# Second products of the late expert units in two blocks instead of four

## Chip, cores and metric

The kernel runs on one core of a Trainium2 chip. The metric is the device time of one execution in microseconds (us), as the median of repeated runs. Matrix products run on TensorE (PE in the profile, its weight loads PEld), elementwise work on VectorE (DVE), ScalarE (ACT) and GpSimd (POOL); SyncE (SP) issues the DMAs.

## The reference, cut to what matters

A sparse attention (4 x 8 heads, 576 tokens, 64 wide) gives `x` with 2304 tokens of 512. Two mixture stages follow; the change lies in the last one:

```python
def _moe2_ref(x, w_gate, w1, w2):
    ...
    for e in range(E):                    # E = 8 experts
        h = np.maximum(x @ w1[e], 0.0)    # 512 -> 1024, the "first products"
        ye = h @ w2[e]                    # 1024 -> 512, the "second products"
        out += P[:, e:e + 1] * ye
    return out
```

## The kernel before, in words

Attention comes first, then the first mixture (24 units "a" and "b"), then 96 expert units. A unit is (e, s, j): expert e of 8, block s of three blocks of 768 tokens, quarter j of the 1024 hidden columns. They are numbered after the 24 units: unit 24 + 32 s + 4 e + j, with s outermost. `Moe.run` (L886) writes out the order of all engines by hand: each engine executes its instructions in the order in which they are issued there.

A unit has seven **slots**. In each slot `mm1` (L684) issues six matmuls of 384 columns into one of two PSUM banks: slots 0, 2 and 4 write `px`, slots 1, 3, 5 and 6 write `py` (`SLOTS`, L521). Slot 2 adds onto what slot 0 left in `px`, and slot 6 onto what slot 5 left in `py`; slots 1, 3, 4, 5 and slot 0 start their bank anew. `combine` (L710) reads the bank after each slot:

- slot 0: ACT copies `px` to `p1` (L716; `p` in the profile).
- slot 1: DVE adds `py` and `p1` into `u2` (L719; `u`).
- slot 2: ACT makes `hh` of `px` (L757), and in slot 3 DVE makes `hl` of `px` (L758).
- slot 3: DVE adds `py` and `u2` into `v` (L722).
- slots 4, 5 and 6: DVE adds the bank and `v` or `u2` into `c` (L736), ACT makes `hh` of `c`, and DVE later makes `hl` of `c` and `hh`, two operands that both lie in SBUF.

So `py` can be started anew in slot 3 only when DVE has read it for `u2`, and `px` can be added to in slot 2 only when ACT has read it for `p1`.

The **second products** of a unit are a queue of 36 matmuls of 512 columns (`queue_d`, L791), which are issued in the next unit, behind the first products of some slots. `pop` (L820) takes a share of the columns left, by the row of `POPS` (L41) that holds for the unit:

```python
POPS = ((1, 1, 1, 1, 1, 2, 1), (0, 2, 0, 2, 0, 3, 1))
...
        n = sum(q[0] for q in self.queue) * share / max(share, self.left)
        self.left -= share
        while self.queue and (n > 0 or not self.queue[0][0]):
...
            self.pops = POPS[u >= 8 * NSB + 16]
```

The second row holds from unit 40 on, which is expert 4 of the first block (the fifth one), to unit 119: 80 units. Its shares 2, 2, 3 and 1 of 8 give blocks of 9, 9, 14 and 4 matmuls behind slots 1, 3, 5 and 6.

When the queue belongs to j = 3, each of the six token tiles ends with `accumulate` (L805), 128x512 on DVE (L816), for expert 0 on ACT instead (L812). `pop` puts these aside in `late`, and at the start of each slot at most two are taken, to be issued at the end of that slot:

```python
                late, self.late = self.late[:2], self.late[2:]
                self.mm1(u, slot)
                ...
                self.pop(slot)
                self.evac(u, slot)
                ...
                for f in late:
                    f()
```

They run in the units with j = 0 and at the start of those with j = 1. Beside all this the weights of the next unit are prepared: `prep1` (L592) on ACT and POOL (L607 to L619), one step in each of slots 0 to 4, and `prep2` (L632), a `w2h` on ACT in slot 3 and a `w2l` on DVE (L642) in slot 5. In the last unit of a block and the first of the next, `xsplit` (L676) adds an `xh` on ACT (L680) and an `xl` on DVE (L681) to slots 0 to 3, and 1 to 3.

Of the kernel before, what the change touches and what calls it, by code (L numbers as in the profile page):

```python
# [37 lines left out]
ORDER = ('wsmTqSfVIviocylrezgxtX', 'msiTSzyVfcqgxwretIXvol', 'imsTSvofwcgIezxltrqyVX', 'TmszVreSviyocxIgfqtlXw', 'mTIVqySvorzseliwcfgxtX', 'msTwVfiSeocyIvgzxlqrtX', 'omTreVfzSqgxwvltXyIcis', 'wmTsSfxvryeiqlVzoIXctg', 'gmTSiVzreIvcofxqlwtsXy', 'miVogTqSvsIcwzyexfrtXl', 'gTmysiSrewfoVcqzxIXtvl', 'VolTsqymiSwcgzfxIvretX', 'mTfoSvcireyszVgxqwtIXl', 'lmszycVTIeoiwfvSgxrtqX', 'ymlTsqwcreVoSfvIzgxtXi', 'moTeSscqzgxyfwVlIvrtXi', 'ymzwoTigSvqxfcreIlsVXt', 'TmSrleIvVzosfcwgxitXqy')  # L38
LOAD_AT, KEYS_AT = 1, 5
PD = 2  # L40
POPS = ((1, 1, 1, 1, 1, 2, 1), (0, 2, 0, 2, 0, 3, 1))  # L41
AHEAD = {-16: 1, -15: 1, -14: 1, -13: 1, -12: 3, -11: 0, -10: 0, -9: 0, -8: 0, -7: 0, -6: 3, -5: 0, -4: 0, -3: 0, -2: 2, -1: 0, 0: 1, 1: 3, 2: 3, 3: 1, 4: 1, 5: 0, 6: 1, 7: 2}
RAMP = 4
CHUNKS = "owooooo3o3o333w3ww3w3w3w3w33ww33ww3ww3ww"
# [471 lines left out]
class Moe:  # L516
# [319 lines left out]
    def gate(self, s, slot):  # L836

        ps = self.xy[0 if slot == 6 else 1]
        t0 = slot - 2
        for tc in (t0, t0 + 1):  # L840
            t = SB * s + 128 * tc
            for d in range(4):
                self.nc.tensor.matmul(ps[:, E * tc:E * tc + E], lhsT=self.x[:, d, t:t + 128], rhs=self.wg[:, d],  # L843
                                      start=d == 0, stop=d == 3, skip_group_check=True)

        def out():
            self.nc.scalar.activation(self.p[:, 6 * s + t0:6 * s + t0 + 2],
                                      ps[:, E * t0:E * t0 + 2 * E].rearrange("p (a b) -> p a b", a=2), AF.Copy)
        return out
# [36 lines left out]
    def run(self):  # L886
        units = self.units
        prep = self.prep1(0)
        for i in range(4):
            self.xsum(0, i, self.nc.vector)  # L890
            next(prep, None)
            yield
        for _ in prep:
            yield
        for slot in range(4):
            while not self.rooms:
                yield
            self.xsplit(0, slot)
            yield
        while self.xy is None or self.pool is None:  # L900
            yield
        sink = None
        gates = {8 * s + (12 if s + 1 < NSB else 9): s for s in range(NSB)}
        for u, (kind, s, j) in enumerate(units):
            nxt = units[u + 1] if u + 1 < len(units) else None
            while u == 1 and self.pool2 is None:
                yield
            if kind != "a":
                self.hs[u] = tuple(self.pool2.tile([128, 2, SB], F32R, tag=t, name=f"{t}{u}", bufs=2)
                                   for t in ("hh", "hl"))  # L910
            ahead = [units[min(u + i, len(units) - 1)][1] for i in range(5)]
            splits, turns = {0: 4, 1: 5, 2: 6} if u == 0 else {}, {}
            if kind == "b" and ahead[1] != s:
                turns = {i + 1: i for i in range(4)}
            elif u and units[u - 1][0] == "b" and units[u - 1][1] != s:
                splits = {i - 3: i for i in range(4, 7)}
            elif ahead[1] != s:
                splits = dict(SPLITS_AT)
            elif u and units[u - 1][1] != s:
                splits = {at - 7: slot for at, slot in SPLITS_AT}  # L920
            prep = self.prep1(u + 1)
            self.load1(u + 2)
            self.pops = POPS[u >= 8 * NSB + 16]
            for slot in range(7):
                yield
                late, self.late = self.late[:2], self.late[2:]
                self.mm1(u, slot)
                gate = self.gate(gates[u], slot) if u in gates and slot in (2, 4, 6) else None
                if sink:
                    try:  # L930
                        sink.send(self.xy[0 if slot in (2, 4, 5) else 1])
                    except StopIteration:
                        sink = None
                self.pop(slot)
                self.evac(u, slot)
                if gate:
                    gate()
                    if u == 8 * NSB + 1 and slot == 6:
                        sink = self.sinkhorn()
                        next(sink)  # L940
                for f in late:
                    f()
                if slot in splits:
                    self.xsplit(ahead[1], splits[slot])
                next(prep, None)
                at = 4 if u == 7 else 1
                if u < 8 and slot in (at, at + 1):
                    self.keep(u, slot - at)
                if slot in turns:
                    self.xturn(u // 8 if kind == "b" else u // 8 - 1, turns[slot])  # L950
                if kind in ("a", "b"):
                    if slot in XSUMS.get(u % 8, ()):
                        self.xsum(NEXT_SB[u // 8], u % 8 - 2 + XSUMS[u % 8].index(slot), self.nc.vector)
                    for at, x in STAGED.get(u % 8, ()):
                        if slot == at:
                            self.xstage(u // 8, x, at // 3 % 2)
                elif slot == 5 and ahead[4] != s:
                    self.xsum(ahead[4], next(i for i in range(4) if ahead[3 - i] == s), self.nc.gpsimd)
                if slot in (3, 5):
                    self.prep2(u + 1 if kind == "a" else u, (slot - 3) // 2)  # L960
            while self.later:
                self.later.pop(0)()
            if kind == "b":
                self.queue_b(u)
                self.left = (2 if nxt[0] == "a" else 1) * sum(self.pops)
            elif kind != "a":
                self.queue_d(u)
                self.left = sum(self.pops)
        self.left = 0
        self.pop(6)  # L970
        for f in self.late:
            f()
# [64 lines left out]
```

## Time and profile before

| | |
|---|---|
| Median of 3 runs | 2189.16 us (2189.15 to 2190.59) |
| The profiled execution | 2189.07 us, span 2187.3 us |
| TensorE | 2150.1 us busy, 98% of the span |
| DVE, ACT, POOL | 58%, 43%, 48% |
| Granted TensorE clock | 1.00 |
| Expert units, first matmul of unit 24 to the end | from 676.4 us on |

The span runs from the first to the last instruction; the time of the execution is 1.8 us longer. Rows of the timeline give start, duration, engine, line, and out<-in of an instruction, all in us from the start of the span. The duration of a matmul holds its way through the array, which overlaps with the next one, so the pace of TensorE is read from the distance between starts.

### The profile page before, as it was taken

What the parts mean: (1) busy time and instruction counts of PE and PEld (TensorE: products, weight loads), DVE (VectorE), ACT (ScalarE), POOL (GpSimd) and SP (SyncE); (2) the same over time, 40 slices, a digit from 0 to 9 for tenths busy, and PEclk for the clock granted to TensorE, in tenths of its full rate; (3) what the DMA queues carried; (4) which work ended last, traced back from release to release, by engine and by line L of the source; (5) the groups of instructions that cost most, each with busy time, mean ns of one, the idle gap of its engine ahead of it and who ended that gap; (6) DMA issues with size and microseconds to landing.
All of it is one profiled execution on the core that took longest, in us unless ns stands there. A gap on an engine that the chain in (4) does not pass through costs nothing.

```text
span 2187.3 us, 31994 instructions
## 1 busy us (share of the span) xinstructions
PE 2150.1 (98%) x12496; PEld 1872.5 (86%) x12496; DVE 1274.8 (58%) x2122; ACT 948.0 (43%) x1770; POOL 1042.4 (48%) x1018
## 2 busy tenths in 40 slices
PE   7999999999999999999999999999999999999999
PEld 4666666899999899999998999999998999999998
DVE  7888888765555654454556445454546444545454
ACT  7888887442324333333334333333334333333332
POOL 6665657740003444444456545454456444444441
PEclk9999999999999999999999999999999999999999
DMA  4333442775552212121212121212112221212121
GB/s 154 105 128 123 133 139 86 260 264 188 222 199 105 78 58 77 59 77 59 77 58 93 72 77 58 77 59 77 64 72 73 92 72 63 77 59 78 58 77 39
DMA packets 64183, 218.09 MB, mean 100 GB/s; under 512 B 6944, under 2 KB 11040, under 8 KB 64032
## 3 DMA queue, kind: packets, MB, share of 16 engines
q1 hardware_dynamic: 64032, 216.05, 28.0%
q8 instruction: 98, 1.61, 0.3%
q14 instruction: 53, 0.43, 0.1%
HBM read 185.61 MB, written 30.41 MB: 99 GB/s over the span
## 4 chain that ended last, share of the span: by engine, by line
PE 90%; DVE 7%; ACT 2%; issue 1%; POOL 0%; DMA 0%; SPq 0%; ACTq 0%; DVEq 0%; POOLq 0%
PE ye L762 40%; PE py L692 22%; PE px L692 17%; PE s L143 4%; PE pv L241 2%; PE t L187 2%; DVE p L162 2%; DVE nmx L147 2%; PE w L474 1%; DVE cva L506 1%; PE py L843 0%; PE tt L198 0%; ACT e L155 0%; DVE cva L503 0%; PE rb L271 0%
## 5 line engine op out<-in xcount | busy, mean ns | idle before, releaser
L762 PE MATMUL ye<-w2l,hh 128*128 128x512 f32 x1152 | 450.6, 391 | 0.0
L762 PE MATMUL ye<-w2h,hl 128*128 128x512 f32 x1152 | 450.5, 391 | 0.0
L762 PE MATMUL ye<-w2h,hh 128*128 128x512 f32 x1152 | 449.6, 390 | 0.0
L757 ACT ACTIVATE hh<-c 128x384 fp32r<-128x384 f32 x288 | 151.2, 526 | 621.4 <-DVE c L736 621.4
L619 POOL TENSOR_TENSOR w1l<-wt,w1h 128x1024 fp32r<-128x1024 f32 x104 | 253.2, 2434 | 267.2 <-ACT w1h L616 267.1
L692 PE MATMUL py<-xh,w1h 128*128 128x384 f32 x960 | 322.6, 336 | 2.4 <-DVE c L736 1.2
L692 PE MATMUL py<-xh,w1l 128*128 128x384 f32 x960 | 322.1, 336 | 0.0
L692 PE MATMUL py<-xl,w1h 128*128 128x384 f32 x960 | 321.9, 335 | 0.0
L614 POOL TENSOR_TENSOR w1l<-raw,w1h 128x256 fp32r<-128x256 f32 x104 | 80.4, 773 | 471.2 <-ACT w1h L608 457.8
L762 PEld LDWEIGHTS ye<-w2h,hl 128*128 128x128 f32 x1152 | 216.2, 188 | 40.5
L762 PEld LDWEIGHTS ye<-w2l,hh 128*128 128x128 f32 x1152 | 216.3, 188 | 35.3 <-DVE w2l L642 0.3
L692 PE MATMUL px<-xh,w1h 128*128 128x384 f32 x720 | 242.0, 336 | 1.5 <-ACT p L716 1.5
L762 PEld LDWEIGHTS ye<-w2h,hh 128*128 128x128 f32 x1152 | 216.3, 188 | 30.7
L692 PE MATMUL px<-xl,w1h 128*128 128x384 f32 x720 | 241.6, 336 | 0.0
L692 PE MATMUL px<-xh,w1l 128*128 128x384 f32 x720 | 241.5, 335 | 0.0
L607 POOL TENSOR_TENSOR wt<-raw 128x512 f32<-128x512 f32 x104 | 140.8, 1354 | 198.0 <-DMA raw<-in_e 183.0
L758 DVE SCALAR_TENSOR_TENSOR hl<-c,hh 128x384 fp32r<-128x384 f32 x288 | 189.3, 657 | 9.5
L692 PEld LDWEIGHTS py<-xh,w1h 128*128 128x128 f32 x960 | 180.3, 188 | 14.8 <-DVE c L736 3.5
L692 PEld LDWEIGHTS py<-xl,w1h 128*128 128x128 f32 x960 | 180.3, 188 | 7.7
L736 DVE TENSOR_TENSOR c<-px,v 128x384 f32<-128x384 f32 x108 | 60.0, 556 | 212.8 <-PE px L692 212.7
L692 PEld LDWEIGHTS py<-xh,w1l 128*128 128x128 f32 x960 | 180.3, 188 | 0.0
L758 DVE SCALAR_TENSOR_TENSOR hl<-px,hh 128x384 fp32r<-128x384 f32 x96 | 53.4, 556 | 215.5 <-ACT hh L757 215.4
(144 smaller groups left out, 3941.0 us busy)
## 6 DMA issues: line engine op xcount, KB each, us to landing
raw<-in_e SPq DMA_DIRECT2D x192, 512.0 KB, 4.0
wraw<-in_w SPq DMA_DIRECT2D x32, 512.0 KB, 4.0
w1h<-w_kept SPq DMA_DIRECT2D x16, 896.0 KB, 5.2
w1l<-w_kept SPq DMA_DIRECT2D x16, 896.0 KB, 7.0
rq<-in_qk SPq DMA_DIRECT2D x15, 576.0 KB, 5.7
w_kept<-w1h SPq DMA_DIRECT2D x8, 896.0 KB, 8.2
w_kept<-w1l SPq DMA_DIRECT2D x8, 896.0 KB, 9.3
raw<-w SPq DMA_DIRECT2D x12, 512.0 KB, 3.6
```

The source lines that it names most:

```text
L143: nc.tensor.matmul(out[:, c, 0:KH], lhsT=q[rows, g, cols], rhs=kk[rows, g], start=True, stop=True)
L147: nc.vector.tensor_reduce(out=nmx[:, s % 18:s % 18 + 1], in_=ps[:, :, 0:288], axis=AX.XY, op=ALU.max, negate=True)
L162: nc.vector.scalar_tensor_tensor(out=ppool[g][:, i, 0:S].rearrange("p (a b) -> p a b", a=2), in0=ps[:, :, 0:288], scalar=thr[:, s % 18:s % ...
L187: nc.tensor.transpose(ps[:, c], p[:, 128 * c:128 * c + 128], k.ident)
L607: nc.gpsimd.tensor_tensor(out=t[:, 0:2], in0=raw[:, 1:3], in1=raw[:, 0:2], op=ALU.subtract)
L614: nc.gpsimd.tensor_tensor(out=wl[:, 0], in0=raw[:, 0], in1=f32(wh[:, 0]), op=ALU.subtract)
L619: nc.gpsimd.tensor_tensor(out=wl[:, 3:7], in0=t, in1=f32(wh[:, 3:7]), op=ALU.subtract)
L692: self.nc.tensor.matmul(out, lhsT=w[:, wi, o], rhs=x[xi][:, d], start=n == 0 and not adds, stop=n == 5, skip_group_check=True)
L736: tt(out=c, in0=src, in1=add, op=ALU.add)
L757: nc.scalar.activation(hi, src, AF.Relu)
L758: self.later.append(lambda: nc.vector.scalar_tensor_tensor(out=lo, in0=src, scalar=0.0, in1=f32(hi), op0=ALU.max, op1=ALU.subtract))
L762: self.queue.append((out.shape[-1], lambda: self.nc.tensor.matmul(out, lhsT=l, rhs=r, start=start, stop=stop, skip_group_check=True)))
```

## The change

The second row of `POPS` gets shares 4.5 and 3.5 behind slots 3 and 5 (the fourth and sixth slot) and none elsewhere. 18432 columns x 4.5 / 8 are 10368, so the first block takes 21 matmuls of 512 columns, the second the other 15. As this row has no share in slot 6 any more, the flush behind the last unit takes the first row.

```diff
-POPS = ((1, 1, 1, 1, 1, 2, 1), (0, 2, 0, 2, 0, 3, 1))
+POPS = ((1, 1, 1, 1, 1, 2, 1), (0, 0, 0, 4.5, 0, 3.5, 0))
...
-        self.left = 0
+        self.left, self.pops = 0, POPS[0]
         self.pop(6)
```

## Rows read from the trace of the kernel before

**Rows 1.** The page: 40 slices of the span (busy tenths, clock), the chain by engine.
```profile
PE   7999999999999999999999999999999999999999
...
PEclk9999999999999999999999999999999999999999
...
PE 90%; DVE 7%; ACT 2%; issue 1%; POOL 0%; DMA 0%; SPq 0%; ACTq 0%; DVEq 0%; POOLq 0%
```

**Rows 2.** Windows: length, busy time (instructions) of PE, PEld, DVE, ACT, POOL; clock; DMA.
```profile
809.39:933.76 124.37, 124.37 (x625) 112.39 (x624) 60.29 (x99) 42.24 (x73) 57.91 (x48) 1.00 0.20 68
933.76:1181.76 248.00, 248.00 (x1249) 224.73 (x1248) 128.62 (x187) 87.29 (x148) 128.66 (x99) 1.00 0.19 68
...
1181.76:1197.95 16.19, 15.93 (x79) 13.90 (x78) 14.03 (x18) 7.37 (x12) 10.26 (x8) 1.00 0.32 114
```

**Rows 3.** Timeline of PE, units 64 and 65: last matmuls of slot 6 and slot 0.
```profile
1320.86 0.34 PE L692 MATMUL py<-xh,w1l 128*128 128x384 f32 x1
...
1322.81 0.34 PE L692 MATMUL px<-xh,w1l 128*128 128x384 f32 x1
```

**Rows 4.** Timeline of DVE from the end of unit 64 into unit 65.
```profile
1321.23 0.56 DVE L736 TENSOR_TENSOR c<-py,u 128x384 f32<-128x384 f32 x1 [0.88 <-PE py L692]
1321.70 0.55 DVE L758 SCALAR_TENSOR_TENSOR hl<-c,hh 128x384 fp32r<-128x384 f32 x1
1322.17 0.74 DVE L816 SCALAR_TENSOR_TENSOR acc<-ye,prob,acc 128x512 f32<-128x512 f32 x1
1322.83 0.55 DVE L758 SCALAR_TENSOR_TENSOR hl<-c,hh 128x384 fp32r<-128x384 f32 x1
1323.30 1.40 DVE L816 SCALAR_TENSOR_TENSOR acc<-ye,prob,acc 128x512 f32<-128x512 f32 x2
1324.62 0.55 DVE L719 TENSOR_TENSOR u<-py,p 128x384 f32<-128x384 f32 x1
```

**Rows 5.** Timeline of PE, unit 1, which has no second products between its slots.
```profile
400.23 0.34 PE L692 MATMUL py<-xh,w1l 128*128 128x384 f32 x1
...
401.27 0.34 PE L692 MATMUL px<-xh,w1l 128*128 128x384 f32 x1
...
402.48 0.34 PE L692 MATMUL px<-xh,w1h 128*128 128x384 f32 x1
...
403.52 0.34 PE L692 MATMUL py<-xh,w1h 128*128 128x384 f32 x1
...
407.46 0.44 PE L692 MATMUL py<-xh,w1h 128*128 128x384 f32 x1 [0.65 <-DVE c L736]
```

**Rows 6.** Timeline of DVE: unit 1, unit 55, and the end of unit 63.
```profile
402.74 0.56 DVE L719 TENSOR_TENSOR u<-py,p 128x384 f32<-128x384 f32 x1 [1.57 <-PE py L692]
...
406.85 0.56 DVE L736 TENSOR_TENSOR c<-py,v 128x384 f32<-128x384 f32 x1
...
1169.70 0.55 DVE L719 TENSOR_TENSOR u<-py,p 128x384 f32<-128x384 f32 x1
...
1301.97 0.90 DVE L758 SCALAR_TENSOR_TENSOR hl<-c,hh 128x384 fp32r<-128x384 f32 x1
```

**Rows 7.** Timeline of POOL: the end of unit 63, the start of unit 65.
```profile
1301.71 0.74 POOL L610 TENSOR_TENSOR wt<-raw,wt 128x256 f32<-128x256 f32 x1
1302.53 0.93 POOL L613 TENSOR_TENSOR wt<-raw,wt 128x256 f32<-128x256 f32 x1
...
1324.12 0.75 POOL L614 TENSOR_TENSOR w1l<-raw,w1h 128x256 fp32r<-128x256 f32 x1 [5.33 <-ACT w1h L608]
```

**Rows 8.** Timeline of ACT: units 55, 60 to 61, and 65.
```profile
1167.57 0.49 ACT L716 ACTIVATE p<-px 128x384 f32<-128x384 f32 x1 [0.90 <-PE px L692]
...
1259.82 0.53 ACT L757 ACTIVATE hh<-c 128x384 fp32r<-128x384 f32 x1 [3.17 <-DVE c L736]
1260.25 0.67 ACT L812 ACTIVATE acc<-ye,prob 128x512 f32<-128x512 f32 x1
...
1323.25 0.49 ACT L716 ACTIVATE p<-px 128x384 f32<-128x384 f32 x1 [0.90 <-PE px L692]
```

## The prediction

> **What bounds the kernel now.** I read the page first. The chain that ended last is TensorE's for 90% [rows 1], so only what changes TensorE's pace, or makes it wait, moves the time. Then the windows of the stretch that the change touches: sixteen units from 933.76 to 1181.76 us take 248.00 us, 15.50 each, and TensorE is busy in all 248.00 [rows 2]. There is no wait to remove. The eight units before them, which run on the other row of `POPS` with seven blocks a unit, take 124.37 us, 15.55 each, also without a gap [rows 2]. The same 78 matmuls thus cost 0.047 us more with seven blocks than with four: 0.0155 us for each block. That is all that blocks cost by themselves.
>
> Last I read the timelines around the start of a unit, since the change takes the cover away there. In the kernel before, 4 second products lie between slot 6 and slot 0, and 9 between slot 1 and slot 2. In the kernel after, slots 6, 0, 1, 2 and 3 stand back to back: 4 x 6 matmuls after slot 6 and slot 3 begins.
>
> **The change, part by part.** All offsets count from T, the start of the last matmul of slot 6.
>
> *Fewer blocks.* Two of four go in each of 80 units: 80 x 2 x 0.0155 = 2.5 us saved. Each matmul, weight load, elementwise instruction and DMA is still issued, the same number of times. SP's loads keep their place in the unit; the output DMAs move with their accumulations by a slot or so, and the loads behind them are needed a unit later, so that costs nothing while that unit of 15.5 us lasts. POOL's queue is not reordered; its steps only start with ACT's copies, and what they make is needed a unit later.
>
> *Where slots 0 to 3 would start.* Unit 1 is a unit without second products, so its slots already stand as the change puts them: from T = 400.23 the last matmul of slot 0 starts at 401.27, slot 2 at 402.48 and slot 3 at 403.52 [rows 5]. That is T + 1.04, T + 2.25 and T + 3.29, with no wait.
>
> *Units that follow no accumulation (58 of 80, the two at the edges set aside).* `u2` must be ready before slot 3. In unit 1 it ran from T + 2.51 to T + 3.07 [rows 6], 0.22 us before slot 3. In the late units the DVE queue ahead of it is `c`, `hl`, `hl`, which are done by about T + 2.1 (`c` starts at T + 0.37, the two `hl` follow, 0.55 each, the last held until `hh` is made) [rows 3, 4, 8]. I cost these at nothing; the cover is those 0.2 us.
>
> *Units that follow an accumulation (j = 1).* Here lies the cost. Behind slot 6 the DVE of the kernel before issues `c`, `hl`, one accumulation, `hl`, two accumulations, and only then `u2`, which starts at 1324.62, T + 3.76 with T = 1320.86, and ends at T + 4.31 [rows 3, 4]. Nobody notices, since nine second products stand between slot 1 and slot 2. The change keeps three accumulations there: the last three tiles end in the block of 15 behind slot 5, slot 6 takes two of them and the next unit's slot 0 the third. The order becomes `c`, `hl`, `acc`, `acc`, `hl`, `acc`, `u2`; the sum of the intervals is the same 3.39 us from `c` to `u2`, and DVE has no gap in it. So `u2` ends at T + 4.31 or later, while slot 3 would start at T + 3.29. TensorE waits there with everything behind it: slot 3, then the block of 21.
>
> *One more delay in that chain.* With slot 0 right behind slot 6, ACT's `p1` starts 0.44 after slot 0's last matmul [rows 3, 8], at T + 1.48, and POOL's L614 starts 0.87 after `p1` [rows 7, 8], at T + 2.35, until T + 3.10. In the kernel before it came at T + 3.26, behind the second `hl`. Now this `hl` starts at T + 2.63 (0.37 + 0.47 + 0.47 + 0.66 + 0.66 from the starts in [rows 4]), inside L614. A pair of the kind is in the trace: an `hl` that started 0.26 into POOL's L610 took 0.90 and ended 0.42 after it, in place of 0.55, and POOL's next, L613, took 0.93 meanwhile [rows 6, 7]; so DVE gets its turn before the POOL instruction behind. Hence `hl` ends at T + 3.52 and not at T + 3.18, `u2` at T + 4.65. The Trainium skill's page "SBUF — State Buffer", section "Who interferes with whom", says that a VectorE instruction with two SBUF operands and a GpSimd one that reads SBUF exclude each other, and that the second blocks until the first is through. By that rule the whole 0.55 would follow L614, for an `hl` until T + 3.65, 18 x 0.13 = 2.3 us more in the sum; the row shows 0.42, and I take the row.
>
> *The wait itself.* The one like it in unit 1: `c` ended at 407.41 and the matmul that waited started at 407.46, and shows 0.44 where its neighbours show 0.34 [rows 5, 6]. I take 0.05 for the release and 0.10 for the restart. A stall is 4.65 + 0.05 + 0.10 - 3.29 = 1.51 us. Bounds: without the POOL delay and the restart 4.31 + 0.05 - 3.29 = 1.07; with twice the release and restart 1.66. I take 1.51, as each of its parts has a row.
>
> *How many.* Accumulations fall into units 40, 44, ..., 116, so 20 units follow one. For 18 of them it is DVE's: 18 x 1.51 = 27.2 us. Units 61 and 93 follow expert 0, whose accumulations run on ACT, 0.67 each behind an `hh`, the first 0.43 after it [rows 8]. Two of them now precede `p1`: `hh` at T + 0.96 (its `c` ends at T + 0.93), `acc` at 1.39 and 2.06, `p1` at 2.73 to 3.22, and slot 2 needs it at 2.25: 0.97 + 0.15 = 1.1 us each, 2.2 in all (0 if ACT's order hid it).
>
> *Edges.* In units 55 and 87 an `xl` stands ahead of `u2`, which started 2.13 after `p1` [rows 6, 8]: T + 3.61, ending at 4.16, a stall of 4.16 + 0.15 - 3.29 = 1.0 each, 2.0 us. Unit 56 takes 16.19 us, 0.69 above the rest [rows 2], and unit 88 is its twin. One accumulation of the block behind slot 1 leaves the DVE queue before slot 5, so I give back 0.5 of each: -1.0 (between 0 and -1.4).
>
> **Sum:** 27.2 + 2.2 + 2.0 - 2.5 - 1.0 = +27.9 us on the profiled execution's 2189.07, which is 0.09 below the median of the runs shown: **2217 us**, 1.3% slower. With the low stall the sum is 18 x 1.07 + 2.2 + 2.0 - 2.5 - 1.4 = +19.6, 2208.7; with the high one and no return at the edges +31.6, 2220.7.
>
> **Rivals.**
> *The stall does not come, and only the blocks count.* This ends on the other side. The place is the DVE queue between slot 6 and `u2`; it decides at T + 3.24, the latest end of `u2` that slot 3 doesn't feel. If accumulations were through before `c`, the queue would be that of the other units, and the time 2189.07 - 2.5 - 1.0 = 2185.6 if the edges don't stall either. For it: before, this very queue harmed nobody. Against it: the block of 15 ends only one slot before, at most two accumulations are taken in a slot, and the 3.39 us are back to back in the trace. Chance 0.07.
>
> *Every unit stalls a little.* The 58 others have 0.2 us to spare in slot 3, and less than that in slot 1, whose `py` waits for the `c` of slot 6 (T + 0.93, slot 1 at T + 1.21). If `hl` or `hh` came later by 0.4, each would lose some 0.2 us: 58 x 0.2 = 12 us more, 2229. Against it is unit 1, whose slots had just such cover and did not wait [rows 5]. The Trainium skill's page "Perfetto Trace Analysis", section "Matmuls", speaks for it: groups of matmuls should rotate through PSUM banks so that the evacuation of one overlaps the next, and the change stacks five slots on two banks. Chance 0.10.
>
> *The clock falls after the stalls.* TensorE's clock was granted in full in each slice, the first included, in which it was busy for seven tenths only [rows 1]. Stalls of 1.5 us in 62 are less idle time than that; chance 0.02, and no row prices it.
>
> *The change reaches other units than I say.* The words speak of the third expert; the code's unit 40 is the fifth. From the third, two more stalls would come: 2220, inside the range.
>
> **How the numbers follow.** The forecast has 0.81, the rivals 0.07, 0.10 and 0.02. The range reaches from 2206, somewhat below the low stall, to 2224, above the high one and half way into the second rival; it leaves out the first rival and the rest of the second. A measurement of this kernel can tell some 0.2%, 4.4 us, from no change. The first rival at 2185.6 is 0.16% faster, so within it, save for a small chance that more is gained: same 0.06, faster 0.02, slower 0.92.
>
> **What would show it.** The list of waits should have a new row, `py` L692 waiting for DVE's `u` L719, some 20 times, about 1.3 us of idle time each, in the units with j = 1 only, and one of `px` waiting for ACT's `p` in units 61 and 93. Units with j = 0, 2 and 3 should take 15.47 us, those with j = 1 about 17.0. In units with j = 1 the `hl` behind two accumulations should last about 0.9 us, with L614 beside it. The forecast is wrong if that row is missing, if the waits stand in all units, or if the other units do not come down to 15.47.

## The result, and the profile after

The changed kernel takes 2219.19 us (median of 4 runs, 2218.57 to 2219.66) against 2189.66 us of the kernel before beside it: 1.013 times as long, with a 95% interval of 1.0118 to 1.0142. The profiled execution took 2218.57 us, its span is 2216.8 us. The predicted 2217 us stand 2.2 us below the median.

The page of the kernel after, TensorE's row of busy time and the chain (before: [rows 1]):

```profile
PE 2154.1 (97%) x12496; PEld 1872.3 (84%) x12496; DVE 1217.0 (55%) x2122; ACT 946.5 (43%) x1770; POOL 1024.5 (46%) x1018
...
PE 86%; DVE 10%; ACT 2%; issue 1%; DMA 0%; POOL 0%; SPq 0%; ACTq 0%; DVEq 0%; POOLq 0%
```

The number of instructions is the same; TensorE's share of the chain fell from 90% to 86%, and DVE's rose from 7% to 10%. What took TensorE's place is in the list of waits of TensorE from 930 us on (waiting for whom: us in total, times, longest):

```profile
PE py L692 <- DVE u L719: 23.6, 20, 1.2
PE px L692 <- ACT p L716: 1.3, 2, 0.7
```

Both rows are new in this stretch, and there are no others: 20 waits of `py` for `u2`, two of `px` for `p1`. The kernel before has one row there, which is gone, for slot 6 of units 56 and 88:

```profile
PE py L692 <- DVE c L736: 0.5, 2, 0.3
```

The windows put them into units. The first four are units 64 to 67 (j = 0 to 3), then units 55, 56 and 61; the columns are those of [rows 2]:

```profile
1315.68:1331.18 15.50, 15.50 (x79) 14.07 (x79) 7.82 (x13) 5.26 (x9) 7.17 (x6) 1.00 0.13 51
1331.18:1348.16 16.98, 15.75 (x79) 13.99 (x79) 8.00 (x13) 5.26 (x9) 7.46 (x6) 1.00 0.23 80
1348.16:1363.67 15.51, 15.51 (x79) 14.08 (x79) 5.94 (x10) 5.26 (x9) 7.17 (x6) 1.00 0.19 69
1363.67:1379.14 15.47, 15.47 (x79) 14.04 (x79) 5.93 (x10) 5.27 (x9) 7.16 (x6) 1.00 0.20 65
...
1172.70:1189.20 16.50, 15.75 (x80) 14.00 (x79) 13.05 (x14) 8.21 (x13) 11.84 (x7) 1.00 0.12 46
1189.20:1204.71 15.51, 15.51 (x80) 14.08 (x80) 12.67 (x16) 7.46 (x12) 8.15 (x6) 1.00 0.32 119
1268.17:1284.56 16.39, 15.74 (x79) 13.99 (x79) 5.93 (x10) 6.90 (x12) 7.13 (x6) 1.00 0.18 61
```

Of the first four only the unit with j = 1 has a gap: 16.98 us, of which TensorE is busy 15.75. The same window shows the full clock. The cause stands in the timelines of unit 65. DVE of the kernel after, where [rows 4] showed the kernel before:

```profile
1331.39 0.56 DVE L736 TENSOR_TENSOR c<-py,u 128x384 f32<-128x384 f32 x1 [0.90 <-PE py L692]
1331.86 0.55 DVE L758 SCALAR_TENSOR_TENSOR hl<-c,hh 128x384 fp32r<-128x384 f32 x1
1332.33 1.40 DVE L816 SCALAR_TENSOR_TENSOR acc<-ye,prob,acc 128x512 f32<-128x512 f32 x2
1333.64 0.87 DVE L758 SCALAR_TENSOR_TENSOR hl<-c,hh 128x384 fp32r<-128x384 f32 x1
1334.44 0.74 DVE L816 SCALAR_TENSOR_TENSOR acc<-ye,prob,acc 128x512 f32<-128x512 f32 x1
1335.10 0.54 DVE L719 TENSOR_TENSOR u<-py,p 128x384 f32<-128x384 f32 x1
```

POOL in the same stretch:

```profile
1333.36 0.74 POOL L614 TENSOR_TENSOR w1l<-raw,w1h 128x256 fp32r<-128x256 f32 x1 [7.40 <-ACT w1h L608]
1334.05 1.60 POOL L617 TENSOR_TENSOR w1l<-raw,w1h 128x512 fp32r<-128x512 f32 x1
```

And TensorE, the last matmuls of slots 6 and 2, the first two of slot 3:

```profile
1331.01 0.34 PE L692 MATMUL py<-xh,w1l 128*128 128x384 f32 x1
...
1334.13 0.34 PE L692 MATMUL px<-xh,w1l 128*128 128x384 f32 x1
1335.70 0.45 PE L692 MATMUL py<-xh,w1h 128*128 128x384 f32 x1 [1.23 <-DVE u L719]
1335.98 0.34 PE L692 MATMUL py<-xl,w1h 128*128 128x384 f32 x1
```

T is 1331.01. `u2` ends at 1335.64, T + 4.63, and slot 3 starts 0.06 later, where it would have started at T + 3.29. Read the second `hl`: it starts 0.28 into L614, takes 0.87 in place of 0.55 and ends 0.41 after L614 does. Read the restart: the second matmul comes 0.28 after the first, where 0.17 is the pace.

From unit 40 to the end the change adds 28.9 us (1282.5 against 1253.5). By units: 18 x (16.98 - 15.50) = 26.6, units 61 and 93 2 x 0.89 = 1.8, units 55 and 87 2 x 1.00 = 2.0, units 56 and 88 -1.3, all others together -0.2. The 0.6 us that the two executions differ by ahead of unit 40 lie in unit 5, which the change does not touch.

### The profile page after: what moved, and what is told of

It reads as the page before. It is cut to its first block, busy times and chain, and to the rows that moved or that the text cites. A ratio compares the mean times of both kernels' runs of the same rounds, so it can differ in the third digit from the quotient of the medians.

```text
span 2216.8 us, 31994 instructions
## 1 busy us (share of the span) xinstructions
PE 2154.1 (97%) x12496; PEld 1872.3 (84%) x12496; DVE 1217.0 (55%) x2122; ACT 946.5 (43%) x1770; POOL 1024.5 (46%) x1018
## 4 chain that ended last, share of the span: by engine, by line
PE 86%; DVE 10%; ACT 2%; issue 1%; DMA 0%; POOL 0%; SPq 0%; ACTq 0%; DVEq 0%; POOLq 0%
PE ye L762 39%; PE py L692 21%; PE px L692 15%; PE s L143 4%; PE pv L241 2%; PE t L187 2%; DVE p L162 2%; DVE acc L816 2%; DVE nmx L147 1%; PE w L474 1%; DVE hl L758 1%; DVE cva L506 1%; DVE c L736 1%; PE py L843 0%; PE tt L198 0%
## 5 line engine op out<-in xcount | busy, mean ns | idle before, releaser
L614 POOL TENSOR_TENSOR w1l<-raw,w1h 128x256 fp32r<-128x256 f32 x104 | 79.8, 768 | 680.5 <-ACT w1h L608 666.6
L758 DVE SCALAR_TENSOR_TENSOR hl<-c,hh 128x384 fp32r<-128x384 f32 x288 | 168.1, 584 | 9.5
L736 DVE TENSOR_TENSOR c<-py,u 128x384 f32<-128x384 f32 x108 | 60.1, 557 | 171.3 <-PE py L692 171.1
```

The source lines that it names most:

```text
L614: nc.gpsimd.tensor_tensor(out=wl[:, 0], in0=raw[:, 0], in1=f32(wh[:, 0]), op=ALU.subtract)
L736: tt(out=c, in0=src, in1=add, op=ALU.add)
L758: self.later.append(lambda: nc.vector.scalar_tensor_tensor(out=lo, in0=src, scalar=0.0, in1=f32(hi), op0=ALU.max, op1=ALU.subtract))
```

## The experiments

The theory: DVE's three accumulations ahead of `u2` make slot 3 wait, where no second products stand between slots 1 and 3. The first rival: the stacked slots make TensorE wait by themselves. The second, on one term of the sum: no instruction of POOL holds `hl`, and the chain is the sum of its intervals. The ratios are to the kernel before.

**The accumulations behind `u2`.** The blocks stay as the change has them.

```diff
-                late, self.late = self.late[:2], self.late[2:]
+                n = 0 if slot in (6, 0) and self.pops is POPS[1] else 2
+                late, self.late = self.late[:n], self.late[n:]
```

> The change's two blocks stay, but no accumulation is issued in slot 6 or slot 0 of the late units, so the last three of a tile group stand behind u2 on DVE (and behind p1 on ACT). Theory (three accumulations ahead of u2 make slot 3 wait): the 18 stalls of 1.5 us and the 2 of 0.9 go, units with j = 1 take 15.5 us in place of 16.98, 2219.2 - 28.7 = 2190.5 us; the stalls of 1.0 us in units 55 and 87 stay. Rival (five stacked slots on two banks cost the wait, whatever DVE has to do): about 2219, unchanged.

Measured: 2190.5 us, ratio 0.9998 (0.9989 to 1.0007). Its window of unit 65, its waits, and DVE at the start of that unit:

```profile
1326.42:1341.88 15.46, 15.46 (x79) 14.03 (x79) 7.76 (x13) 5.26 (x9) 7.17 (x6) 1.00 0.26 88
```

```profile
PE py L692 <- DVE u L719: 1.5, 2, 0.8
```

```profile
1328.77 0.56 DVE L719 TENSOR_TENSOR u<-py,p 128x384 f32<-128x384 f32 x1 [0.44 <-PE py L692]
1329.24 2.06 DVE L816 SCALAR_TENSOR_TENSOR acc<-ye,prob,acc 128x512 f32<-128x512 f32 x3
```

DVE now waits for TensorE ahead of `u2`, and the three accumulations follow. With the same five slots stacked, units with j = 1 take 15.5 us; the two waits left are those of units 55 and 87. The first rival falls.

**One accumulation a slot,** two ahead of `u2` in place of three:

```diff
-                late, self.late = self.late[:2], self.late[2:]
+                n = 1 if self.pops is POPS[1] else 2
+                late, self.late = self.late[:n], self.late[n:]
```

> At most one accumulation is taken in a slot of the late units, so two stand ahead of u2 in place of three. Theory: u2 starts at T + 3.10 and ends at T + 3.65, the stall is 3.65 + 0.15 - 3.29 = 0.5 us, units with j = 1 take 16.0 us, units 61 and 93 about 15.8; 2219.2 - 18 x 1.0 - 2 x 0.6 = 2200 us. Rival (the stacked slots cost the wait): about 2219.

Measured: 2200.46 us, ratio 1.0046 (1.0031 to 1.0061). Unit 65 and the DVE queue there:

```profile
1326.28:1342.27 15.99, 15.74 (x80) 14.00 (x80) 8.24 (x14) 5.27 (x9) 7.19 (x6) 1.00 0.22 83
```

```profile
1327.42 0.74 DVE L816 SCALAR_TENSOR_TENSOR acc<-ye,prob,acc 128x512 f32<-128x512 f32 x1
1328.09 0.55 DVE L758 SCALAR_TENSOR_TENSOR hl<-c,hh 128x384 fp32r<-128x384 f32 x1
1328.55 0.74 DVE L816 SCALAR_TENSOR_TENSOR acc<-ye,prob,acc 128x512 f32<-128x512 f32 x1
1329.21 0.55 DVE L719 TENSOR_TENSOR u<-py,p 128x384 f32<-128x384 f32 x1
```

None, two and three accumulations ahead of `u2` give 15.46, 15.99 and 16.98 us: the wait goes by the queue. From two to three it grows by 0.99: 0.66 for the accumulation and 0.33 for the `hl`, which here starts before L614 and takes its 0.55.

**The cover given back,** to the units with j = 1 alone; DVE's order ahead of `u2` stays the change's.

```diff
-POPS = ((1, 1, 1, 1, 1, 2, 1), (0, 0, 0, 4.5, 0, 3.5, 0))
+POPS = ((1, 1, 1, 1, 1, 2, 1), (0, 0, 0, 4.5, 0, 3.5, 0), (0, 2, 0, 2, 0, 3, 1))
...
-            self.pops = POPS[u >= 8 * NSB + 16]
+            self.pops = POPS[(u >= 8 * NSB + 16) * (1 + (u % 4 == 1))]
```

> The units with j = 1 get the old row of shares back (blocks of 9, 9, 14 and 4), the others keep the change's two blocks; DVE's order of instructions ahead of u2 in those units stays the change's. Theory (nine second products between slots 1 and 2 cover the accumulations): units with j = 1 take 15.5 us, 2219.2 - 28.4 = 2191 us. Rival (the accumulations ahead of u2 delay TensorE whatever lies between, by bank or by queue): units with j = 1 stay near 17.

Measured: 2190.99 us, ratio 1.0002 (0.9992 to 1.0012); units with j = 1 take 15.50 us in the mean. Unit 65:

```profile
1323.00:1338.51 15.51, 15.51 (x80) 14.04 (x80) 9.66 (x15) 5.40 (x10) 7.70 (x6) 1.00 0.25 81
```

The wait needs both, the queue and the missing cover.

**The `hl` of slot 6 ahead of the accumulations:**

```diff
+                if slot == 6 and self.pops is POPS[1]:
+                    while self.later:
+                        self.later.pop(0)()
                 for f in late:
                     f()
```

> The hl of slot 6 is issued ahead of the accumulations of slot 6, in place of behind them; the number of instructions ahead of u2 is the same. Theory (hl is held by GpSimd's L614): hl starts at T + 1.5, before L614, lasts 0.55 us, u2 ends at T + 4.50 in place of 4.63, units with j = 1 take 16.84 us, 2216.7 us. Rival (no such hold, the chain is only the sum of its intervals): hl must wait for hh until T + 1.5, which leaves DVE a gap of 0.19 us that the other order does not have, so units with j = 1 take 17.17 us, 2222.6 us.

Measured: 2217.86 us, ratio 1.0125 (1.011 to 1.014). The intervals overlap those of the change, so the units decide. Unit 65, and its DVE and POOL:

```profile
1330.11:1346.98 16.87, 15.75 (x79) 13.99 (x79) 7.76 (x13) 5.27 (x9) 7.16 (x6) 1.00 0.23 76
```

```profile
1330.79 1.24 DVE L758 SCALAR_TENSOR_TENSOR hl<-c,hh 128x384 fp32r<-128x384 f32 x2
1331.94 2.06 DVE L816 SCALAR_TENSOR_TENSOR acc<-ye,prob,acc 128x512 f32<-128x512 f32 x3
1333.92 0.55 DVE L719 TENSOR_TENSOR u<-py,p 128x384 f32<-128x384 f32 x1
```

```profile
1332.29 0.74 POOL L614 TENSOR_TENSOR w1l<-raw,w1h 128x256 fp32r<-128x256 f32 x1 [7.42 <-ACT w1h L608]
```

16.87 us against the theory's 16.84 and the rival's 17.17. L614 now lies beside accumulations, which read a PSUM operand, and neither is slowed.

**All three accumulations between the two `hl`,** so that the second meets L617:

```diff
-                late, self.late = self.late[:2], self.late[2:]
+                n = 3 if self.pops is POPS[1] else 2
+                late, self.late = self.late[:n], self.late[n:]
```

> Up to three accumulations are taken in a slot of the late units, so all three stand between the two hl behind slot 6: c, hl, acc, acc, acc, hl, u2; the number ahead of u2 is the change's. Theory (an hl that meets a running GpSimd instruction is held until its end): the second hl would start at T + 3.29, inside L617, which is longer than L614 and ends near T + 4.35; hl ends at T + 4.77, u2 at T + 5.24, the stall is 2.1 us, units with j = 1 take 17.5 us, 2219 + 18 x 0.6 = 2230 us. Rival (only the sum of DVE's intervals counts): u2 ends at T + 4.31, units with j = 1 take 16.65 us, 2213 us.

Measured: 2244.25 us, ratio 1.0253 (1.0237 to 1.0268), 14 us more than the theory and on its side. Unit 45 and unit 65 of this run:

```profile
1013.95:1031.50 17.55, 15.75 (x80) 14.00 (x80) 8.57 (x13) 5.26 (x9) 7.14 (x6) 1.00 0.21 78
1336.04:1355.21 19.17, 17.38 (x80) 15.13 (x79) 8.56 (x13) 5.26 (x9) 7.09 (x6) 0.91 0.21 69
```

DVE and POOL in unit 65:

```profile
1339.16 1.44 DVE L758 SCALAR_TENSOR_TENSOR hl<-c,hh 128x384 fp32r<-128x384 f32 x1
1340.52 0.55 DVE L719 TENSOR_TENSOR u<-py,p 128x384 f32<-128x384 f32 x1
```

```profile
1338.91 1.27 POOL L617 TENSOR_TENSOR w1l<-raw,w1h 128x512 fp32r<-128x512 f32 x1
```

The `hl` meets L617 0.25 after its start, takes 1.44 us and ends 0.42 after it, as forecast; unit 45 takes 17.55 us against 17.5. So the hold by POOL is shown from both sides, and the second rival falls. What the theory did not have is unit 65: 19.17 us, at a granted clock of 0.91. TensorE, from the end of slot 2 on:

```profile
1338.99 0.34 PE L692 MATMUL px<-xh,w1l 128*128 128x384 f32 x1
1341.12 0.44 PE L692 MATMUL py<-xh,w1h 128*128 128x384 f32 x1 [1.79 <-DVE u L719]
...
1342.94 0.63 PE L762 MATMUL ye<-w2h,hl 128*128 128x512 f32 x1
1343.36 0.63 PE L762 MATMUL ye<-w2h,hh 128*128 128x512 f32 x1
...
1346.14 0.40 PE L762 MATMUL ye<-w2l,hh 128*128 128x512 f32 x1
1346.38 0.40 PE L762 MATMUL ye<-w2h,hl 128*128 128x512 f32 x1
```

After 1.79 us of idling and one more slot, second products follow each other at 0.43 us for a while, where 0.23 is the pace at 2.4 GHz; it is the lower level, 1.2 GHz. Nine of the 18 units with this wait take 19.1 to 19.2 us, the other nine 17.5: 9 x 1.6 = 14.4 us, which is the excess over the theory. From unit 40 to the last matmul the granted clock falls nine times, each time 0.3 to 1.4 us after such a wait ended, and nowhere else.

**Seven blocks** in all late units, to price a block where all slots have cover:

```diff
-            self.pops = POPS[u >= 8 * NSB + 16]
+            self.pops = POPS[0]
```

> All late units use the first row of shares: seven blocks of about five, in place of the change's two and the four of before. Theory (a block costs 0.0155 us): 2190.5 + 80 x 3 x 0.0155 = 2194.2 us, units of 15.55 us. By the 0.012 us that the second products of a block lose against their even pace in the trace of the change: 2193.4. Rival (blocks are free, and what differed was the stretch of the program): 2190.5.

Measured: 2192.76 us, ratio 1.0014 (1.0005 to 1.0023), 2.6 us above the median of the kernel before beside it (2190.12). Units 64 to 83, twenty of them, in this run:

```profile
1306.57:1617.50 310.93, 310.93 (x1561) 280.94 (x1560) 138.69 (x231) 105.55 (x181) 143.52 (x120) 1.00 0.19 68
```

They take 310.00 us in the kernel before (20 x 15.50 [rows 2]): 0.93 / 60 = 0.0155 us a block, as in [rows 2]. The price of a block holds between seven and four. That the whole run shows 2.6 us and not 3.7 is due to units 56 and 88, which have no wait here and take 15.6 us in place of 16.2.

**The blocks one slot earlier,** 21 behind slot 2 and 15 behind slot 5:

```diff
-POPS = ((1, 1, 1, 1, 1, 2, 1), (0, 0, 0, 4.5, 0, 3.5, 0))
+POPS = ((1, 1, 1, 1, 1, 2, 1), (0, 0, 4.5, 0, 0, 3.5, 0))
```

> The same two blocks of 21 and 15, behind slots 2 and 5 in place of 3 and 5. Theory (the wait is slot 3's for u2, so a block between slots 2 and 3 covers it): the 18 stalls and the two at the edges go, the two in units 61 and 93, where slot 2 waits for p1, stay with 0.9 us each; 2190.5 us, the same as before. Rival (two blocks cannot cover seven slots): slot 5 waits for v in its place, and the time stays above 2200.

Measured: 2190.9 us, ratio 1.0005 (0.9996 to 1.0014). The waits from 930 us on:

```profile
PE px L692 <- ACT p L716: 1.3, 2, 0.7
PE py L692 <- DVE c L736: 1.1, 2, 0.6
```

The 20 waits for `u2` are gone and the two for `p1` are left. Not forecast were two waits for `c`, in units 56 and 88: there slot 1 waits for the `c` of slot 6 of units 55 and 87, which stands behind an `hl` and a `w2l` on DVE:

```profile
1182.59 2.87 DVE L642 TENSOR_TENSOR w2l<-raw,w2h 128x1024 fp32r<-128x1024 f32 x1
```

This `w2l` lies beside two instructions of POOL and takes 2.87 us, the one of unit 56 in the same run 1.21; the `hl` ahead of it takes 1.51 in place of 0.55. So it is a stretched queue of DVE again.

**The same, without accumulations in slots 6 and 0** (the edits of the first run and of the run just above together):

> The blocks behind slots 2 and 5, and no accumulation in slots 6 and 0. Theory: no stall is left in units 40 to 119, the 0.65 us that units 56 and 88 lost before are gained, and the two blocks fewer save 80 x 0.01 us at most, since slots 1 and 2 give back some of it: 2190.5 - 1.3 - 0.8 = 2188.4 us, 0.1% below before. Rival (the blocks' 0.031 us a unit come in full): 2186.7 us.

Measured: 2189.17 us, ratio 0.9997 (0.9989 to 1.0006). No difference from the kernel before can be told. The only waits left are those for `c`, so the 1.3 us expected from units 56 and 88 did not come (they take 16.3 us). Units 64 to 83:

```profile
1311.33:1621.08 309.75, 309.75 (x1561) 281.04 (x1561) 137.73 (x230) 105.32 (x180) 143.58 (x120) 1.00 0.19 69
```

15.49 us a unit: two blocks fewer give 0.0125 us, not 0.031.

**Units 56 and 88 with the later blocks,** a try to remove those two waits:

```diff
-            self.pops = POPS[u >= 8 * NSB + 16]
+            self.pops = POPS[(u >= 8 * NSB + 16) * (1 + (u in (56, 88)))]
```

with the change's row as a third one, on top of the run before; its limit on accumulations holds for both rows.

> As the run with blocks behind slots 2 and 5 and no accumulation in slots 6 and 0, but units 56 and 88, where slot 6 still waited 0.8 us for c there, have their blocks behind slots 3 and 5, where they took 15.5 us. Theory: no wait is left from unit 40 on; from the start of unit 40 to that of unit 119 it takes 1224.7 - 2 x 0.8 = 1223.1 us, 2.7 less than before, and 2187.5 us in all, 0.12% below before, about as much as the timing can tell. Rival (units 55 or 57 take the wait over): no gain on 1224.7.

Measured: 2190.02 us, ratio 0.9999 (0.999 to 1.0008). Unit 56 here:

```profile
1182.72:1199.42 16.70, 15.99 (x79) 13.96 (x79) 12.90 (x17) 7.37 (x12) 13.43 (x10) 1.00 0.31 111
```

There is no gain, but not for the rival's reason: the wait stays in unit 56 itself, which takes 0.4 us more than in the run before (16.28). The expectation had put the wait at the wrong slot. It is slot 1 that waits, for a `c` that belongs to the unit ahead, so the blocks of unit 56 cannot cover it. No version that beats the kernel before was found.

## Why the prediction was right, and where it was off

*The stall behind an accumulation* came as worked out. `u2` ended at T + 4.63 (forecast 4.65), slot 3 started 0.06 later (0.05), the restart cost 0.11 (0.10), and a unit lost 1.48 us against the 15.50 of before, where 1.51 less the blocks' 0.03 were expected. (The "4 x 6 matmuls" count slot 6 itself: 18 lie between slot 6 and slot 3, and the offsets are right.) That it takes the three accumulations and the missing cover together is shown by the runs that gave back one of them. The term for POOL's hold, 0.34, is 0.32 in the change, and moving the `hl` to either side of L614 moved the unit as the hold would have it: +0.57 us where it meets L617, and -0.11 ahead of L614, where most of the 0.32 goes into waiting for `hh`. By the rule of the Trainium skill's page "SBUF — State Buffer", "Who interferes with whom", the `hl` would end 0.55 after L614; all 18 of these `hl` in the kernel after end 0.42 after it, so the exclusion is there, but the rest after it is shorter than the whole instruction.

*Expert 0's accumulations on ACT* cost 0.89 a unit, not 1.1: the two take 1.25 us together in unit 61, so they follow each other at 0.58, where I had taken the 0.67 that one of them lasts.

```profile
1269.39 1.25 ACT L812 ACTIVATE acc<-ye,prob 128x512 f32<-128x512 f32 x2
```

*The edges* cost 1.0 for each of units 55 and 87, as forecast. Units 56 and 88 gave back 1.3 where 1.0 was forecast, but the reason was wrong, and the number near it by luck. The accumulation that was to leave the queue did no harm in the kernel before: DVE idled for 2.12 us after it (first row). What is different is that slots 1 to 3 come without blocks between them, and slot 4 behind the block of 21. The `xl` ahead of slot 4's `c` ends 9.6 us into the unit, where it ended at 11.7, and DVE idles before it can read slot 4's bank (second row, the kernel after):

```profile
1188.51 0.96 DVE L681 TENSOR_TENSOR xl<-s,xh 128x768 fp32r<-128x768 f32 x1 [2.12 <-ACT xh L680]
...
1199.41 0.56 DVE L736 TENSOR_TENSOR c<-px,v 128x384 f32<-128x384 f32 x1 [0.64 <-PE px L692]
```

*Fewer blocks* is the term that was off: 2.5 us of saving, of which 56 x 0.031 = 1.7 should show in the late units without a stall, and 0.2 does. Units with j = 0, 2 and 3 take 15.50, 15.51 and 15.49 us in the mean. They did not come down to 15.47, and the prediction had named that as a sign of being wrong. The price of a block is right, 0.0155 us, as the run with seven blocks shows. But it was carried over to slots that no longer have cover. Worked out from the starts of all matmuls in 54 units without a stall: the second products lose 27 ns a unit against their even pace, 49 before, and slot 0 loses 3 in place of 9; but slots 1 to 3 lose 26, where they lost 1.5. That is the place of the prediction's second rival, though with some nanoseconds and not with a wait that the profile would list. The run with blocks behind slots 2 and 5 and no accumulation in slots 6 and 0 shows the same: its slots 1 to 3 lose 19, and its slot 3, which has a block ahead of it there, loses 1 in place of 7. What delays these matmuls stays open. A bank that is freed late would hold up the first matmul of a slot, but in slot 1 the loss is spread over all six.

From unit 40 on the sum is thus 1.0 us short (27.9 against 28.9). It is so near because the missing saving, 2.3 us, stands against 1.3 us by which the stalls and the edges cost less than forecast. Of the rest to the 2.2 us, 0.6 lies in unit 5 and 0.6 between the profiled execution and the median.

*The prediction's first rival*, no stall at all, falls with the list of waits. *The clock* stayed at its full level through all stalls of the change, 1.23 us at the longest; what idle times of 1.8 us did to it is told in the last section.

## What to carry to other kernels

Matmuls between two uses of a bank are cover for whatever the evacuating engine has queued, and the units to look at are those in which that queue is longest, not the common ones: here one unit in four paid nearly everything. Where an order is written by hand, putting the work that nobody waits for behind the evacuation (the accumulations behind `u2`) was worth as much here as the cover. A saving per block that was measured with cover did not hold where the cover went.

## What the runs showed of the hardware that was not expected

TensorE's clock fell from 2.4 to 1.2 GHz after idle times of 1.8 us in otherwise dense work, in 9 of 18 such places, while the 18 such places of the kernel after, with 1.2 us of idling each, left it alone. Each fall cost 1.6 us, more than half of the 2.1 us stall that it followed. The Trainium skill's page "TensorE: Matmul & The Clock Gate", section "Why this matters for your kernels", has it that idle gaps between bursts of matmuls bring the clock down; the granted clock of 0.91 in unit 65 of that run agrees in kind. The page warns of longer gaps than these 1.8 us, and here the trace decides. The prediction gave this 0.02, and for the change itself it did not come.

An `hl` that POOL holds needs less than its whole time afterwards: alone it takes 0.55 us, held it ends 0.41 to 0.42 us after the POOL instruction, whether it met it 0.25 or 0.28 us after its start, and whether L614 (0.74 us) or L617 (1.27 us) held it.
